# A recurrence and a mixture of experts on one core: two stretches of mixture a chunk, T sent by chunk, a new order of the beginning

## The chip, the cores and the metric

One core of one Trainium2 chip runs the whole program. The metric is the time of one execution in device microseconds.

## What is computed

Three stages follow each other: a linear recurrence with a matrix state (4 batches x 8 heads, 768 tokens, head size 40), a dense gated layer, and a dense mixture of four experts on its result.

```python
def _attn_ref(r, k, v, w, a, b):
    for t in range(S):
        y[:, :, t] = np.einsum('bhd,bhde->bhe', rt, state)
        Sa = np.einsum('bhde,bhe->bhd', state, at)
        state_decay = state * wt[:, :, None, :] - np.einsum('bhd,bhe->bhde', Sa, bt)
        state = state_decay + np.einsum('bhd,bhe->bhde', vt, kt)

def _moe_ref(x, w_a, w_b, w_out):
    return (x @ w_a * (x @ w_b)) @ w_out

def _moe2_ref(x, domain_probs, w1, w2):
    p = domain_probs / (domain_probs.sum(-1, keepdims=True) + 1e-09)
    for e in range(E):
        out += p[:, e:e + 1] * (np.maximum(x @ w1[e], 0.0) @ w2[e])
```

## The kernel before, in words

The recurrence is worked in chunks of 32 tokens. There are 48 of them: the batches are split into two passes (NPASS), whose chunks alternate, so that chunk n follows on chunk n-2. Four chunks make a group (SUP); a group gives one tile of 256 columns to the first dense layer, which this document calls the mixture (class Moe1): per tile 12 blocks of 24 matmuls in a pair of l1 (16) and l2 (8).

A chunk needs these steps, all methods of Att. `decay` (L130) scans the decays to R, `inverse` (L138, L140) takes the reciprocal gam, `scale` (L149, L152) multiplies k and b by R into a tile ke, and a by gam into A. `prep_T` (L170, L174) makes the matrix T of a chunk and transposes k and b; VectorE masks a half of it (L177), ScalarE copies the other half to tbs (L179) and the transposes to L (L182). T of a chunk must be inverted with ones on the diagonal: `invert` does it for a whole group at once, on 128 partitions, in 31 pairs of an elementwise multiply (L203) and a subtract (L206). Half of the partitions hold the even columns of an inverse and half the odd ones. For that T goes through DRAM: two stores of a group's tbs to td, issued by ScalarE (L190), two loads to tblk (L195) and one of the start values X (L197), issued by SP. `place` stores X to DRAM (xd, L215) and loads it as xr in another layout (L218). `settle` copies xr to xs on ScalarE (L225), with even and odd columns interleaved.

Then come `rhs` (L304, a copy to rh on ScalarE L308), `u` (L324, reads xs; ScalarE and VectorE write its result to G, L328, L330), and `sy` (L347: new state, VectorE L355, and output ys, L359). Beside them lie, for later chunks, `tr` (L290, transposes the state; copy S, L293), `q` (L274, copy L278) and `cf` (L253, mask L257). rhs, u and sy all use the PSUM buffer with tag "B", prep_T the one with tag "A".

The order of all engines is written by hand in `body`. From chunk 4 on the loop puts per chunk: rhs with tr, a stretch of mixture `moe(g[0])`, u with q, `moe(g[1])`, sy with cf, T of chunk n + LEAD, and `moe(g[2])`. The counts are matmuls: 18, 26, 22 up to chunk 7, then 20, 28, 24. In a group's first chunk settle stands ahead of u, and after u `split` (L422, L423) cuts the tile of the group before into a high and a low part; `moe` doesn't enter a tile before that (`ready`). At a group's last chunk place follows u. `mo.load` sends ys through DRAM (L516 store xt, L520 and L522 loads xf).

The weights of the mixture come by `Moe1.fetch`, issued by ScalarE (L453), 1.9 MB for two of twelve blocks. `convert` (L496 to L509) turns them to a high and a low part in steps, on VectorE, ScalarE and GpSimd; `fill` takes such steps. In the beginning, the chunks' inputs e1 are fetched into buffers of their own or of tiles that are used later (E1); T of chunks 0 to 3 is made, the first inverse is taken on VectorE, T of 4 to 7 is made among its steps; the second inverse is taken on GpSimd, as all later ones are. After the loop the rest of the mixture runs, and then the experts (Moe2, L694 to L716).

Of the kernel before, what the change touches and what calls it, by code (L numbers as in the profile page):

```python
# [19 lines left out]
C = 32  # L20
NCH = S // C
NPASS = 2
# [15 lines left out]
NK = (128, 104)  # L38

# [34 lines left out]
E1 = ("e1", "ys", "tblk1", 0, 1, "e1", "ys", "e1")  # L74


class Att:
# [3 lines left out]
    def __init__(self, ctx, tc, e1, e2, vt, cst):  # L81
# [23 lines left out]
        self.pre, self.sup, self.e2, self.S, self.rh = {}, {}, {}, {}, {}  # L105
# [12 lines left out]
    def fetch(self, n):  # L118
        tag = E1[n] if n < RING else "e1"
        if tag in (0, 1):  # L120
            e1 = self.L[tag][:104, SUP:].rearrange("p i a d -> p (i a d)")[:, :1032]
        else:
            e1 = self.pool.tile([104, 1032], F32, tag=tag, name=f"e1_{n}", bufs=1)[:]
        self.nc.sync.dma_start(e1, self.e1d[n])
        self.pre[n] = e1
# [8 lines left out]
    def inverse(self, n):  # L134
        nc, pool = self.nc, self.pool
        e1, R = self.pre[n]
        gam = pool.tile([104, 8, 32], F32, tag="gam", name=f"gam_{n}", bufs=RING + 1)
        nc.vector.reciprocal(gam[:], R[:, :, 1:33])  # L138
        lc = pool.tile([104, 8, 1], F32, tag="lc", name=f"lc_{n}", bufs=RING)
        nc.scalar.copy(lc[:], R[:, :, 32:33])  # L140
        self.pre[n] = e1, R, gam, lc

    def scale(self, n, eng):
# [4 lines left out]
        ke = self.pool.tile([104, 8, 2, 32], F32, tag="ke", name=f"ke_{n}")  # L148
        eng.tensor_tensor(out=ke[:], in0=kb, in1=R[:, :, 0:32].unsqueeze(2).to_broadcast([104, 8, 2, 32]), op=ALU.mult)  # L149
# [3 lines left out]
        self.pre[n] = lc, gam, ke  # L153

    def prep_T(self, n, tag="A"):
# [5 lines left out]
        if cc == 0:  # L161
            self.sup[s] = pool.tile([128, SUP * 8, 32], F32, tag="tbs", name=f"tbs_{s}", bufs=1)
        tbs = self.sup[s]
# [11 lines left out]
        for P in range(2):  # L175
            kr, br = (slice(x[P], x[P] + 32) for x in (KROW, BROW))
# [7 lines left out]

    def invert(self, s, eng):

        nc, pool = self.nc, self.pool
        td = self.dr.tile([SUP * 8, 2, 32, 32], F32, tag="td", name=f"td_{s}")
        for P in range(2):
            nc.scalar.dma_start(td[:, P].rearrange("a j t -> j a t"), self.sup[s][BROW[P]:BROW[P] + 32])  # L190
        yield
        tb = pool.tile([128, 32, 32], F32, tag=f"tblk{s % 2}", name=f"tblk_{s}", bufs=1)
        src = td[:].rearrange("a v j t -> (a v) (j t)")
        for z in range(2):
            nc.sync.dma_start(tb[64 * z:64 * z + 64].rearrange("p j t -> p (j t)"), src)  # L195
        X = pool.tile([128, 32, 16], F32, tag=f"xx{s % 2}", name=f"xblk_{s}", bufs=1)
        nc.sync.dma_start(X[:], self.x0d)  # L197
        yield
        for k in range(31):
            m, c = 31 - k, k // 2 + 1  # L200
            tm = pool.tile([128, 136], F32, tag="tmp0" if s == 0 else "tmp", name=f"tmp_{s}_{k}")
            t = tm[:, :m * c].rearrange("p (j c) -> p j c", c=c)
            eng.tensor_tensor(out=t, in0=tb[:, k + 1:, k:k + 1].to_broadcast([128, m, c]),  # L203
                                    in1=X[:, k:k + 1, :c].to_broadcast([128, m, c]), op=ALU.mult)
# [5 lines left out]
    def place(self, s):  # L210
# [5 lines left out]
        xr = pool.tile([128, 2, SUP * 4, 16], F32, tag=f"xx{s % 2}", name=f"xr_{s}", bufs=1)  # L216
        for z in range(2):
            nc.sync.dma_start(xr[:, z], xd[z].rearrange("a p c -> p a c"))  # L218
        self.sup[s] = xr

    def settle(self, s):
        nc, pool, xr = self.nc, self.pool, self.sup[s]
        xs = pool.tile([128, SUP * 4, 16, 2], F32, tag="xs", name=f"xs_{s}", bufs=1)
        for z in range(2):
            nc.scalar.copy(xs[:, :, :, z], xr[:, z])  # L225
        self.sup[s] = xs
# [84 lines left out]
    def u(self, n, tag="B", also=None):  # L311
# [4 lines left out]
        xs = self.sup[s]  # L316
# [3 lines left out]
        for j in range(4):  # L320
            for z in range(2):
                for P in range(2):
                    b = band(z, P)
                    nc.tensor.matmul(U[rows[P], z, j], xs[b, 4 * cc + j].rearrange("p c z -> p (c z)"), rh[b, j], start=True, stop=True)  # L324
# [4 lines left out]
        for P, br in enumerate(rows):  # L329
            nc.vector.tensor_tensor(out=g_t(G[P][br]), in0=p_t(ps[br]),  # L330
                                    in1=self.um[br].unsqueeze(1).unsqueeze(1).to_broadcast([32, 2, 4, 32]), op=ALU.mult)
        next(more, None)

    def sy(self, n, ys, tag="B", also=None):
# [15 lines left out]
        yield  # L350
        m = n + NPASS
        if m < N:
# [4 lines left out]
        yield  # L357
        for P, o in enumerate(rows):
            nc.vector.tensor_tensor(out=ys[o, :, cc].rearrange("p (j z) t -> p z j t", z=2), in0=p_t(ps[o]),  # L359
                                    in1=gam[o].rearrange("p (j z) t -> p z j t", z=2), op=ALU.mult)  # L360
# [6 lines left out]
def consts():  # L367
    c = np.zeros((128, CST_N), np.float32)
    tri = np.tril(np.ones((32, 32), np.float32), -1)
# [33 lines left out]
def pack_att(r, k, v, w, a, b):  # L403
    ch = {n: _chunks(x) for n, x in dict(r=r, k=k, v=v, w=w, a=a, b=b).items()}
    em = {n: _emajor(ch[n], 0, 0.0) for n in "kab"}
# [23 lines left out]
class Moe1:  # L429
# [16 lines left out]
    def fetch(self, i):  # L446
# [357 lines left out]
def general(tc, e1, e2, cst, wab, w2d, wo, probs, w1, w2, out):  # L804
# [4 lines left out]
    with ExitStack() as c:  # L809
        dram = c.enter_context(tc.tile_pool(name="gdram", bufs=1, space=DRAM))  # L810
        x2 = dram.tile([NS, 128, 3, 256], F32, name="x2g")
        with ExitStack() as ctx:
            mo = Moe1(ctx, tc, wab, w2d, wo, {}, True)
            for i in range(0, mo.NK1, 2):
                mo.fetch(i)
# [28 lines left out]
            with tc.For_i(0, NS, 1) as s:  # L844
                ys = pool.tile([104, 8, SUP, 32], F32, tag="ys", name="gys", bufs=1)
                for step in range(2):
# [19 lines left out]
                    for t in range(31, -1, -1):  # L866
# [3 lines left out]
                        tt(dv[:], eye, wide(E2[:, :, 1, :, t]), ALU.mult)  # L870
# [7 lines left out]
                        for z in range(2):  # L878
                            tt(x[:, z], Sa[z], kb[:, z, 1, :, t].unsqueeze(2).to_broadcast(full[:1] + full[2:]), ALU.mult)
                        tt(S[:], S[:], x[:], ALU.subtract)  # L880
                        V = total(dv, "V")
                        for z in range(2):
                            tt(x[:, z], V[z], kb[:, z, 0, :, t].unsqueeze(2).to_broadcast(full[:1] + full[2:]), ALU.mult)
# [31 lines left out]
def body(ctx, tc, e1, e2, vt, cst, wab, w2d, wo, probs, w1, w2, out):  # L915
# [6 lines left out]
    with ExitStack() as ca:  # L922
# [55 lines left out]
        for n in range(SUP):  # L978
            fetch(n)
        for n in range(NPASS):  # L980
            at.loade(n)
            at.loadv(n)
        at.loadv(2)
        at.ones(0)
        for n in range(SUP, RING - 1):
            fetch(n)
        for n in range(3):
            prep(n, pool)
        for n in range(SUP):
            at.prep_T(n, "AB"[n % 2])  # L990
            if n == SUP - 1:
                inv = at.invert(0, v)
                steps(1)
            if n + 3 < RING - 1:
                prep(n + 3, pool)
        at.ones(1)
        steps(1)
        fetch(7)
        mo.fetch(0)
        at.prep_T(4, "A")  # L1000
        steps(14)
        at.prep_T(5, "B")
        prep(7, pool)
        steps(20)
        at.prep_T(6, "A")
        steps(14)
        at.prep_T(7, "B")
        inv0, inv = inv, at.invert(1, pool)
        steps(1)
        whole(inv0)  # L1010
        at.place(0)
        steps(1)
        mo.fetch(2)
        both(at.cf(0), at.cf(1))
        at.loade(2)
        at.loade(3)
        at.rhs(0, "A")
        at.rhs(1, "B")
        whole(at.cf(2))
        fill(4)  # L1020
        steps(12)
        at.settle(0)
# [3 lines left out]
        fill(2)  # L1026
        y0, y1 = at.sy(0, ys, "A"), at.sy(1, ys, "B")
        both(y0, y1)
        at.loadv(3)
        mo.fetch(4)  # L1030
        steps(8)
        whole(at.tr(2, None, "A"))
        whole(at.tr(3, None, "B"))
        fill(4)
        whole(at.q(2))
        whole(at.q(3))
        at.rhs(2, "A")
        whole(at.cf(3))
        at.rhs(3, "B")
        at.loade(4)  # L1040
        at.loadv(4)
        at.loade(5)
        fill(6)
        steps(12)
        at.u(2, "A")
        at.u(3, "B")
        fill(2)
# [3 lines left out]
        fetch(8)  # L1051
        mo.fetch(6)
        steps(12)
        fill(4)
        both(at.cf(4), at.cf(5))
        whole(at.tr(4, None, "A"))
        whole(at.q(4))
        fill(6)
        mo.split(0)
        steps(100)  # L1060
        at.place(1)
        prep(8, v)
        at.prep_T(8)
        fetch(9)
        for i in range(8, mo.NK1, 2):
            mo.fetch(i)
        ready = 1
        for n in range(SUP, N):
            s, cc = divmod(n, SUP)
            m = n + LEAD  # L1070
            g = (18, 26, 22) if n < RING else (20, 28, 24)
            at.rhs(n, "B", n + 1)
            if n + 2 < N:
                if n > SUP + 1:
                    at.loade(n + 2)
                if n > SUP:
                    at.loadv(n + 2)
            if n == SUP:
                at.loade(n + 2)
                prep(9, v)  # L1080
                fetch(10)
            elif n == SUP + 1:
                at.loade(n + 2)
                prep(11, v)
                fetch(12)
            elif m < N:
                at.inverse(m)
                at.scale(m, v)
                fetch(m + 1)
            moe(g[0])  # L1090
            if n < SUP + 2:
                at.prep_T((9, 11)[n - SUP])
            if n == SUP + 1:
                inv, every = at.invert(2, pool), 2
                steps(2)
            if cc == 0:
                at.settle(s)
            at.u(n, "B", n + 1)
            if cc == 3 and s + 1 < N // SUP:
                steps(100)  # L1100
                at.place(s + 1)
                every = 0
            if cc == 0 and s > 1:
                mo.split(s - 1)
                ready += 1
            if n < SUP + 2:
                prep((10, 12)[n - SUP], v)
                fetch((11, 13)[n - SUP])
# [84 lines left out]
```

## Time and profile before

| | us |
|---|---|
| median of 3 runs (lowest to highest) | 1729.84 (1723.58 to 1734.29) |
| the profiled execution | 1729.1 |
| its span | 1727.3 |
| TensorE busy | 1463.6 |
| VectorE, ScalarE, GpSimd busy | 837.6, 593.2, 406.3 |
| mean granted clock of TensorE | 0.935 |

The span goes from the first to the last instruction. Matmuls are pipelined, so TensorE's busy time is that in which at least one is under way; PEld is its loading of weights. SPq and ACTq are the queues' own instructions, DMA issues above all; "x2" counts merged instructions. The number in brackets is the engine's idle time before the instruction, and what ended it.

### The profile page before, as it was taken

To read this page: it belongs to the slowest core of one execution; us is meant where nothing else is said; L and a number is where in the kernel's file an instruction comes from. 1 tells how busy PE (TensorE), PEld (TensorE's weight loads), DVE (VectorE), ACT (ScalarE), POOL (GpSimd) and SP (SyncE) were. 2 spreads that over 40 slices of the span, in tenths; PEclk is the share of its full clock that TensorE was granted. 3 is DMA by queue.
4 is the path that set the end of the run, shared out by engine and by line. 5 is a ranking of instruction groups with operands and counts; after the bars stand their busy time and mean duration, and the time that the engine had idled before them with its cause. 6 is when DMAs were issued, how large, how long until landed. Compare 5 with 4: busy or idle time off the path is not lost.

```text
span 1727.3 us, 40183 instructions
## 1 busy us (share of the span) xinstructions
PE 1463.6 (85%) x17202; PEld 1326.5 (77%) x17202; DVE 837.6 (48%) x1631; ACT 593.2 (34%) x1450; POOL 406.3 (24%) x794
## 2 busy tenths in 40 slices
PE   4144657988978889889889999999999999999998
PEld 3144657877877878778778887777899999999997
DVE  6564875655756556566534454445322322232222
ACT  2132334333434334443433466664211211121111
POOL 5162380522605325144150220002000200010000
PEclk9975778988999889999999999999999999999999
DMA  8445214332342323432321466557200100000000
GB/s 197 92 137 130 71 29 88 76 85 66 86 105 68 82 61 93 98 76 77 73 57 28 148 179 162 149 155 237 70 1 0 57 12 1 1 1 16 31 16 33
DMA packets 142623, 135.81 MB, mean 79 GB/s; under 512 B 94628, under 2 KB 112484, under 8 KB 142436
## 3 DMA queue, kind: packets, MB, share of 16 engines
q1 hardware_dynamic: 113012, 117.99, 25.8%
q10 hardware_dynamic: 29424, 15.17, 3.4%
q8 instruction: 137, 2.24, 0.6%
q14 instruction: 50, 0.41, 0.1%
HBM read 115.03 MB, written 18.09 MB: 77 GB/s over the span
## 4 chain that ended last, share of the span: by engine, by line


## 5 line engine op out<-in xcount | busy, mean ns | idle before, releaser
L563 PE MATMUL l<-xh,w 128*128 128x256 f32 x1440 | 316.5, 303 | 34.1 <-ACT xh L422 33.0
L698 DVE SCALAR_TENSOR_TENSOR hl<-l,hh 128x512 fp32r<-128x512 f32 x192 | 132.3, 690 | 344.0 <-ACT hh L697 343.8
L563 PEld LDWEIGHTS l<-xh,w 128*128 128x128 f32 x1440 | 255.2, 208 | 37.8 <-ACT xh L422 34.5
L563 PE MATMUL l<-xl,w 128*128 128x256 f32 x864 | 263.7, 311 | 0.1
L697 ACT ACTIVATE hh<-l 128x512 fp32r<-128x512 f32 x192 | 114.0, 595 | 396.0 <-PE l L694 396.0
L711 PE MATMUL o<-h,hh 128*128 128x320 f32 x768 | 239.1, 311 | 9.7 <-ACT hh L697 6.1
L713 PE MATMUL o<-h,hl 128*128 128x320 f32 x768 | 239.9, 313 | 5.1 <-DVE hl L698 4.9
L203 POOL TENSOR_TENSOR tmp<-tblk,xblk 128x126 f32<-128x126 f32 (+22 forms) x341 | 139.0, 408 | 424.3 <-DMA xblk<-cst 320.5
L712 PE MATMUL o<-l,hh 128*128 128x320 f32 x768 | 236.9, 309 | 0.0
L563 PEld LDWEIGHTS l<-xl,w 128*128 128x128 f32 x864 | 179.5, 208 | 6.2 <-DVE xl L423 2.1
L423 POOL TENSOR_TENSOR l<-r,h 128x512 fp32r<-128x512 f32 (+1 forms) x32 | 46.7, 1483 | 575.6 <-ACT h L422 575.6
L711 PEld LDWEIGHTS o<-h,hh 128*128 128x128 f32 x768 | 144.2, 188 | 26.1 <-ACT hh L697 14.5
L713 PEld LDWEIGHTS o<-h,hl 128*128 128x128 f32 x768 | 144.0, 188 | 12.2 <-DVE hl L698 11.6
L206 POOL TENSOR_TENSOR xblk<-xblk,tmp 128x126 f32<-128x126 f32 (+22 forms) x341 | 145.9, 428 | 26.9 <-POOL tmp L203 0.2
L694 PE MATMUL l<-XL,h 128*128 128x512 f32 x384 | 151.7, 395 | 0.0
L694 PE MATMUL l<-XH,h 128*128 128x512 f32 x384 | 151.5, 395 | 0.0
L694 PE MATMUL l<-XH,l 128*128 128x512 f32 x384 | 150.0, 391 | 0.0
L712 PEld LDWEIGHTS o<-l,hh 128*128 128x128 f32 x768 | 144.2, 188 | 6.7
L170 PE MATMUL psT<-A,ke 40*64 40x32 f32 x1536 | 67.0, 240 | 64.1 <-DVE A L152 28.4
L567 DVE TENSOR_TENSOR g<-l,a 128x256 f32<-128x256 f32 x144 | 60.7, 421 | 116.4 <-ACT a L565 116.2
L170 PEld LDWEIGHTS psT<-A,ke 40*64 40x64 f32 x1536 | 60.7, 158 | 67.9 <-issue 36.2
L179 ACT COPY tbs<-psT 32x256 f32<-32x256 f32 x96 | 35.0, 365 | 219.5 <-DVE A L177 217.1
(119 smaller groups left out, 2643.3 us busy)
## 6 DMA issues: line engine op xcount, KB each, us to landing
g<-e SPq DMA_DIRECT2D x48, 419.2 KB
e<-e SPq DMA_DIRECT2D x46, 419.2 KB
e<-e SPq DMA_DIRECT2D x48, 208.0 KB
wr<-wab ACTq DMA_DIRECT2D x12, 512.0 KB
tblk<-td SPq DMA_DIRECT2D x24, 256.0 KB
r<-w SPq DMA_DIRECT2D x8, 768.0 KB
gx<-wab SPq DMA_DIRECT2D x12, 512.0 KB
r<-w SPq DMA_DIRECT2D x8, 640.0 KB
```

Source lines behind the costliest of these rows:

```text
L170: nc.tensor.matmul(T[P][KROW[P]:KROW[P] + 64, a], ke[r, a].rearrange("p y t -> p (y t)"), self.A[P][r, k, a], start=True, stop=True)
L203: eng.tensor_tensor(out=t, in0=tb[:, k + 1:, k:k + 1].to_broadcast([128, m, c]), in1=X[:, k:k + 1, :c].to_broadcast([128, m, c]), op=ALU.mult)
L206: eng.tensor_tensor(out=X[:, k + 1:, :c], in0=X[:, k + 1:, :c], in1=t, op=ALU.subtract)
L423: eng.tensor_tensor(out=lo, in0=raw, in1=hi, op=ALU.subtract)
L563: nc.tensor.matmul(o, l, r, start=j == 0, stop=j == len(ops) - 1)
L567: nc.vector.tensor_tensor(out=g[:], in0=ps[:, 256:512], in1=a[:], op=ALU.mult)
L694: nc.tensor.matmul(ps[:], l, r, start=i == 0, stop=i == len(ops) - 1)
L697: nc.scalar.activation(hh[:], ps[:], AF.Relu)
L698: nc.vector.scalar_tensor_tensor(out=hl[:], in0=ps[:], scalar=0.0, in1=hh[:], op0=ALU.max, op1=ALU.subtract)
L711: nc.tensor.matmul(o[:], hh[:, s], h2[:, k], start=first, stop=False)
L712: nc.tensor.matmul(o[:], hh[:, s], lo2[:, k], start=False, stop=False)
L713: nc.tensor.matmul(o[:], hl[:, s], h2[:, k], start=False, stop=last)
```

## The change

Tokens of k, v and b stand in a chunk with the even positions ahead of the odd ones (ORD), so that an inverse can be used as its two halves lie, and settle is gone. scale works in place on e1, with two instructions for k and b. T goes to DRAM by chunk, in four stores and two loads, all issued by SP; X's start values are loaded apart. In the loop T of chunk n + 7 is made between rhs and u, sy uses the PSUM buffer "A" and, from chunk 2 on, writes ys ahead of the state, and the mixture has two stretches a chunk: 28 and 20 matmuls up to chunk 7, then 44 and 28. place stands at the start of a group's last chunk, split ahead of sy in its first one. Weights are fetched by SP, and the beginning has a new order. The program that is taken for other inputs (`general`) follows the new order of tokens.

```diff
+ORD = [*range(0, C, 2), *range(1, C, 2)]
-E1 = ("e1", "ys", "tblk1", 0, 1, "e1", "ys", "e1")
+E1 = ("e1", "e1", "e1", 0, 1, "tblk1", "ys", "e1")
...
-        ke = self.pool.tile([104, 8, 2, 32], F32, tag="ke", name=f"ke_{n}")
-        eng.tensor_tensor(out=ke[:], in0=kb, in1=R[:, :, 0:32].unsqueeze(2).to_broadcast([104, 8, 2, 32]), op=ALU.mult)
+        for y in range(2):
+            k = kb[:, :, y].rearrange("p a (z c) -> p a z c", z=2)
+            eng.tensor_tensor(out=k, in0=k, in1=R[:, :, 0:32].rearrange("p a (c z) -> p a z c", z=2), op=ALU.mult)
...
-            nc.scalar.copy(tbs[br, 8 * cc:8 * cc + 8], T[P][br])
+            nc.scalar.copy(tbs[br], T[1 - P][br])
+        for P in (1, 0):
+            for z in range(2):
+                o = BROW[P] + 16 * z
+                nc.sync.dma_start(td[8 * cc:8 * cc + 8, P].rearrange("a (c z) t -> z c a t", z=2)[z], tbs[o:o + 16])
+        yield
...
+    def loadt(self, n):
+        src = td[8 * cc:8 * cc + 8].rearrange("a v j t -> (a v) (j t)")
+        for z in range(2):
+            r = 64 * z + 16 * cc
+            self.nc.sync.dma_start(tb[r:r + 16].rearrange("p j t -> p (j t)"), src)
+    def loadx(self, s):
+        X = self.pool.tile([128, 32, 16], F32, tag=f"xx{s % 2}", name=f"xblk_{s}", bufs=1)
+        self.nc.sync.dma_start(X[:], self.x0d)
...
     def invert(self, s, eng):
-        for P in range(2):
-            nc.scalar.dma_start(td[:, P].rearrange("a j t -> j a t"), self.sup[s][BROW[P]:BROW[P] + 32])
-        for z in range(2):
-            nc.sync.dma_start(tb[64 * z:64 * z + 64].rearrange("p j t -> p (j t)"), src)
-        nc.sync.dma_start(X[:], self.x0d)
...
-        for z in range(2):
-            nc.sync.dma_start(xr[:, z], xd[z].rearrange("a p c -> p a c"))
+        yield
+        for r in (slice(0, 4), slice(4, 16)):
+            for z in range(2):
+                nc.sync.dma_start(xr[:, r, z], xd[z, r].rearrange("a p c -> p a c"))
-    def settle(self, s):
-        for z in range(2):
-            nc.scalar.copy(xs[:, :, :, z], xr[:, z])
...
-    def fetch(self, i):
+    def fetch(self, i, eng):
-            self.nc.scalar.dma_start(raw[:], src[:, m * at:m * at + m])
+            eng.dma_start(raw[:], src[:, m * at:m * at + m])
```

The new beginning, in the order of its steps: fetch 0 to 2, inputs of chunks 0 and 1, fetch 3 to 6 and loadx(0) among them; prep (decay, inverse, scale on GpSimd) of 0 to 5 with T of 0 to 3 and their loadt between; loadv(2), mo.fetch(0), prep of 6 and 7, fetch 8 and 9; cf of 0 and 1, 16 steps of the first inverse (on VectorE), the cf masks, mo.fetch(2), rhs of 0 and 1, the rest of the inverse, its store; T(4), the load xr, T(5) to T(7) with loadt of 4 to 7 between; prep of 8 and 9; cf(2); then u of 0 and 1, with steps of the second inverse (GpSimd) and of the weights' conversion between, and on as before. mo.fetch(4) follows sy of 0 and 1, mo.fetch(6) sy of 2 and 3, and T(8). After the second inverse and its place come 24 matmuls of mixture, mo.fetch(8) and (10), T(9), fetch 12, prep 10, 16 matmuls, T(10), prep 11, 8 matmuls.

```diff
         for n in range(SUP, N):
-            g = (18, 26, 22) if n < RING else (20, 28, 24)
+            g = (28, 20) if n < RING else (44, 28)
+            if cc == 3 and s + 1 < N // SUP and n > RING:
+                whole(at.place(s + 1))
+            if SUP + 1 < n + 2 < N and n > SUP - 1 and n + 2 > 5:
+                at.loadv(n + 2)
             at.rhs(n, "B", n + 1)
...
-            moe(g[0])
-            if cc == 0:
-                at.settle(s)
-            at.u(n, "B", n + 1)
+            rest = ()
+            if m < N:
+                rest = at.prep_T(m)
+                next(rest)
+                fetch(m + 3)
+                if m % SUP == SUP - 1:
+                    at.loadx(m // SUP)
+            if m + 1 < N:
+                at.decay(m + 1)
+            at.u(n, "B", n + 1, rest)
+            if cc == 3 and n < RING:
+                whole(inv)
+                whole(at.place(s + 1))
+            if n + 3 < N:
+                at.loade(n + 3)
+            moe(8)
+            if m + 1 < N:
+                at.inverse(m + 1)
+            if m < N:
+                at.loadt(m)
+                if m % SUP == SUP - 1:
+                    inv, every = at.invert(m // SUP, pool), 2
+                    if n >= RING:
+                        whole(inv)
+            moe(16)
+            if m + 1 < N:
+                at.scale(m + 1, v)
+            moe(g[0] - 24)
             if cc == 0 and s > 1:
                 mo.split(s - 1)
+            whole(at.sy(n, ys, "A", n + 2))
+            if cc == 0 and s > 1:
                 ready += 1
             if cc == SUP - 1:
                 mo.load(s, ys)
-            if m < N:
-                at.prep_T(10 if n == SUP else m)
-            moe(g[2])
+            moe(g[1])
```

## Rows read from the trace of the kernel before

**Rows 1.** Busy time by stretch: us, PE, PEld, DVE, ACT, POOL, clock, DMA share, GB/s.

```profile
0.00:272.40 272.40, 127.87 (x2232) 117.26 (x2232) 176.60 (x333) 79.01 (x222) 122.52 (x203) 0.78 0.43 107
272.40:833.70 561.30, 482.75 (x8953) 445.73 (x8954) 345.88 (x701) 225.50 (x659) 206.65 (x496) 0.93 0.34 82
833.70:957.00 123.30, 108.14 (x1869) 100.58 (x1869) 51.72 (x122) 45.06 (x120) 23.81 (x62) 0.93 0.21 51
957.00:1727.30 770.30, 744.86 (x4157) 662.98 (x4155) 263.43 (x476) 243.61 (x450) 53.28 (x33) 0.99 0.24 71
```

**Rows 2.** Timeline at a group's first chunk: start, duration, engine, instruction.

```profile
630.15 1.18 PE L324 MATMUL psU<-rh,xs 32*32 32x72 f32 x32 [3.28 <-ACT xs L225]
...
634.65 1.02 ACT L422 CAST xh<-xf 128x256 fp32r<-128x256 f32 x3
```

**Rows 3.** Busy time in two stretches of 2 us, columns as in rows 1.

```profile
600.00:602.00 2.00, 2.00 (x19) 2.00 (x18) 1.47 (x3) 1.04 (x4) 1.76 (x4) 1.00 0.81 229
...
638.00:640.00 2.00, 2.00 (x11) 2.00 (x10) 0.36 (x1) 0.37 (x1) 0.00 (x0) 0.50 0.00 0
```

**Rows 4.** Waits of the whole run: us in total, times, longest.

```profile
PE psY L347 <- ACT G L278: 27.3, 24, 3.8
```

**Rows 5.** Timeline of TensorE: T in one chunk, then chunk 41.

```profile
603.74 1.12 PE L170 MATMUL psT<-A,ke 40*64 40x32 f32 x32
605.16 0.38 PE L563 MATMUL l<-xl,w 128*128 128x256 f32 x1
...
869.91 0.71 PE L304 MATMUL psR<-G,A 128*32 128x72 f32 x32
...
870.93 0.38 PE L563 MATMUL l<-xl,w 128*128 128x256 f32 x1
...
873.50 0.70 PE L324 MATMUL psU<-rh,xs 32*32 32x72 f32 x32
...
874.57 0.39 PE L563 MATMUL l<-xh,w 128*128 128x256 f32 x1
...
878.11 1.20 PE L347 MATMUL psY<-G,L 128*40 128x72 f32 x32
...
879.62 0.39 PE L563 MATMUL l<-xl,w 128*128 128x256 f32 x1
```

**Rows 6.** Timeline of SP's queue over two chunks and the next group's start.

```profile
603.45 2.30 SPq L238 DMA_DIRECT2D G<-vt  x2
...
616.97 1.13 SPq L215 DMA_DIRECT2D xd<-xblk  x2
620.97 1.47 SPq L218 DMA_DIRECT2D xr<-xd  x2
622.53 1.45 SPq L516 DMA_DIRECT2D xt<-ys  x2
628.20 0.38 SPq L520 DMA_DIRECT2D xf<-xt  x1
```

**Rows 7.** GpSimd's inverse of one group, by line; then two rows of the timeline.

```profile
L206 POOL TENSOR_TENSOR xblk<-xblk,tmp 128x126 f32<-128x126 f32 (+22 forms) x31 | 13.8, 444 | 2.4
L203 POOL TENSOR_TENSOR tmp<-tblk,xblk 128x126 f32<-128x126 f32 (+22 forms) x31 | 12.3, 395 | 43.2 <-DMA xblk<-cst 40.9
...
611.83 0.80 POOL L203 TENSOR_TENSOR tmp<-tblk,xblk 128x78 f32<-128x78 f32 x1
612.71 0.40 POOL L206 TENSOR_TENSOR xblk<-xblk,tmp 128x78 f32<-128x78 f32 x1
```

**Rows 8.** Timeline of the beginning, one row of each engine that waited.

```profile
44.25 0.20 DVE L203 TENSOR_TENSOR tmp<-tblk,xblk 128x31 f32<-128x31 f32 x1 [11.07 <-DMA xblk<-cst]
...
91.21 2.14 PE L324 MATMUL psU<-rh,xs 32*32 32x72 f32 x64 [4.15 <-ACT xs L225]
...
137.10 0.58 PE L563 MATMUL l<-xh,w 128*128 128x256 f32 x1
...
152.86 0.40 ACT L308 COPY rh<-psR 128x288 f32<-128x288 f32 x1 [14.49 <-issue]
```

More of the change, by code (lines that the diff above doesn't have):

```diff
@@ L309, in rhs, with u @@
         next(more, None)
[L311 removed]
+    def u(self, n, tag="B", also=None, between=()):
         nc, rh = self.nc, self.rh.pop(n)
@@ L331, in u, with sy @@
                                     in1=self.um[br].unsqueeze(1).unsqueeze(1).to_broadcast([32, 2, 4, 32]), op=ALU.mult)
+        for _ in between:
+            pass
         next(more, None)
-    def sy(self, n, ys, tag="B", also=None):
+    def sy(self, n, ys, tag="B", also=None, first="y"):
         nc = self.nc
@@ L350, in sy, with y @@
         yield
+        def y():
+            for P, o in enumerate(rows):
+                nc.vector.tensor_tensor(out=ys[o, :, cc].rearrange("p (j z) t -> p z j t", z=2), in0=p_t(ps[o]),
+                                        in1=gam[o].rearrange("p (j z) t -> p z j t", z=2), op=ALU.mult)
         m = n + NPASS
+        if first == "y":
+            y()
+            yield
         if m < N:
@@ L356, in sy @@
                                         in1=lc[o].rearrange("p (j z) o -> p z j o", z=2).to_broadcast([40, 2, 4, 40]), op=ALU.mult)
[L357 to L360, printed above, removed]
+        if first != "y":
+            yield
+            y()
         next(more, None)
@@ L996, in body, with mix @@
[L996 to L1002, printed above, removed]
-        prep(7, pool)
[L1004 to L1014, printed above, removed]
+        def mix(k, f=4):
+            for _ in range(k):
+                steps(f)
+                fill(1)
@@ new lines, in T @@
+        def T(n, tag):
+            whole(at.prep_T(n, tag))
+        for n in range(3):
+            fetch(n)
+        at.loade(0)
+        at.loadv(0)
+        fetch(3)
+        at.loade(1)
+        at.loadv(1)
+        at.ones(0)
+        fetch(4)
+        fetch(5)
+        at.loadx(0)
+        fetch(6)
+        prep(0, pool)
+        prep(1, pool)
+        prep(2, pool)
+        T(0, "A")
+        fetch(7)
+        prep(3, pool)
+        T(1, "B")
+        at.loadt(0)
+        prep(4, pool)
@@ L1015, in body @@
+        T(2, "A")
+        at.loadt(1)
+        prep(5, pool)
+        T(3, "B")
+        at.loadt(2)
+        at.loadt(3)
+        at.loadv(2)
+        mo.fetch(0, nc.sync)
+        prep(6, pool)
+        prep(7, pool)
+        fetch(8)
+        fetch(9)
+        inv = at.invert(0, v)
+        c0, c1 = at.cf(0, at.bank("psC_0", "A")), at.cf(1, at.bank("psC_1", "B"))
+        next(c0)
+        next(c1)
+        steps(16)
+        both(c0, c1)
         at.loade(2)
         at.loade(3)
+        mo.fetch(2, nc.sync)
@@ L1017, in body @@
         at.rhs(0, "A")
         at.rhs(1, "B")
+        whole(inv)
+        put = at.place(0)
+        next(put)
+        T(4, "A")
+        whole(put)
+        at.ones(1)
+        T(5, "B")
+        at.loadt(4)
+        T(6, "A")
+        at.loadt(5)
+        T(7, "B")
+        at.loadt(6)
+        at.loadx(1)
+        at.loadt(7)
+        fetch(10)
+        prep(8, pool)
+        prep(9, pool)
         whole(at.cf(2))
-        fill(4)
-        steps(12)
-        at.settle(0)
+        inv = at.invert(1, pool)
@@ L1023, in body @@
+        steps(4)
         ys = newys(0)
```

167 lines of the change are left out of this document (60 added, 107 removed).

## The prediction, made before the changed kernel was run

> **What bounds the kernel now.** I read the table of stretches first [rows 1]. The program has three parts: a beginning up to 272.4 us, when chunk 8 of the recurrence starts; the loop over the other chunks up to 957 us; and the tail, 770.3 us, in which TensorE is busy 744.9 us and the recurrence is over. In the beginning TensorE is busy for 127.9 of 272.4 us, in the eight groups of four chunks (chunks 8 to 39) for 482.8 of 561.3, which is 70.2 us a group, in the last eight chunks for 108.1 of 123.3. No other engine is near full there: VectorE has 345.9 us for 32 chunks, 10.8 each. So the loop waits. The second view, the timeline at a first chunk of a group, shows where [rows 2]: TensorE stood 3.28 us until ScalarE had copied the inverses (xs), and after that the mixture waited until ScalarE split the new tile (xh, from 634.65). The third, two-microsecond stretches, shows what follows [rows 3]: the granted clock is 0.50 at 638 to 640, the 1.2 GHz level, and 11 mixture matmuls fit in place of 19. The fourth adds smaller waits: sy stood 27.3 us in 24 waits until ScalarE had read the PSUM buffer that it shared with u [rows 4].
>
> **What a chunk costs when nothing waits.** Chunk 41 shows it [rows 5]: rhs and tr 869.91 to 870.93, 1.02; 20 mixture matmuls 2.57; u and q 1.07; 28 matmuls 3.54; sy and cf 1.51. The two stretches of mixture differ by 8 matmuls and 0.97, so a matmul is 0.121 and coming in and out of the mixture 0.15. A chunk that also prepares another one has 1.42 for T and K (603.74 to 605.16). Before: 72 x 0.121 + 3 x 0.15 + 1.02 + 1.07 + 1.51 + 1.42 = 14.2. A group would be 56.7 of its 70.2.
>
> **The change in the loop, part by part.**
> - Two stretches of mixture, not three: one entry less, 0.15, so 14.0 a chunk, 56 a group. What lay in the first stretch covered ScalarE's copy of rh. Now T and K cover it (1.42 against a copy of about 0.4 and S of 0.4). In chunks 41 to 47 no T is left: about 0.65 of wait opens, bounds 0 and 1.2; such a chunk is 12.76 - 0.15 + 0.65 = 13.25.
> - sy moves to the other PSUM buffer: the wait of [rows 4] goes. What sy needs next is VectorE's masked t rows; by the durations of the groups they come some 2.5 us ahead of it, since 44 matmuls (5.3 us) lie between.
> - No copies of the inverses: 0.8 of ScalarE a group and, above all, the wait for a place in ScalarE's order, 3.28 [rows 2]. u now waits for the load itself. That is issued at the start of chunk 3 of a group and not after its u, a whole chunk (15) ahead of use.
> - The new tile is first wanted after sy of the group's first chunk instead of straight after u. That is the first stretch of mixture (5.3) and sy (1.5) later, and what each such stall costs now, some 11.5 us (two waits of about 3.2 and 10 us at half speed, of which 5 are lost), should shrink to 2, bounds 0 and 11.5. At the low bound the tile is there; at the high one all that [rows 2, 3] show stays.
> - Scaling k and b in two instructions instead of one, in place: about 0.2 more VectorE a chunk. VectorE then has 11.0 in 14 to 15 us; it is covered, with 3 us of slack. Without that cover it costs its 0.2.
> - ys before state in sy: state is 0.86 later, but tr wants it after 28 matmuls and rhs, 4 us on. Nothing, or 0.86 if VectorE is late.
> - T by chunk: SP gets four small writes and two reads a chunk, beside two loads of v, one of e1, one of e2. The waits that this adds are for T in SBUF and for the landing of T, and behind them stand all other loads. This makes a ring, whose time for a group I add up [rows 6, 7]: GpSimd's 62 steps 12.3 + 2.4 + 13.8 + 2.3 = 30.8; store of X 1.13 and its landing 2.87; the load xr 2.2; v 1.3; T 1.8; e1 and e2 0.8; wait for T 1.5, read 0.8; xt 1.45 and its landing 4.2 at most, 3.5 taken; xf 1.5; v, T, e1, e2, x0 again 4.5; wait and read 1.8; landing 2.4. Without GpSimd that is 27.6; the pieces of T, which no row has, are taken at 0.45 each, between xf's first at 0.38 and xd's two at 0.57 (bounds 0.31 and 1.15). GpSimd's step beside VectorE's scaling took 0.80 and the next one 0.40 [rows 7]. VectorE is denser after the change, so I take 32 for 30.8 (bounds 30.8 and 36, the steps stretched in the ratio of the two VectorE shares). The ring then has 59.6 against 56 + 2 on TensorE. I take **60 us a group**, 57 to 66.
> The Trainium skill, GPSIMD Engine Reference, section Specifications, says that GpSimd's SBUF interface is shared with VectorE and contended by VectorE instructions with two SBUF inputs. By it all scaling and subtracting of VectorE would stretch the steps, some 33 us of GpSimd as an estimate and 61 a group; the trace agrees in the pair named, 0.80 against 0.40.
>
> **The beginning.** The rows of now [rows 8]: the first inverse starts at 44.25 after 11.07 of waiting for its input; u of chunk 0 at 91.21; the mixture at 137.10; and ScalarE's copy of rh at 152.86 after 14.49 in which its queue only issued weight loads. After the change:
> - The inputs of the first inverse go chunk by chunk and its start values early, so it starts when T of chunk 3 is there, about 32. It now takes 25.6, to 69.84, of which 6.2 are masks and preparation between its steps; 19.4 and the cf masks, 1.7, end it at 53.
> - Then T of chunks 4 to 7 and the preparation of 8 and 9 lie ahead of u: 4 x 1.7 + 2 x 2.5 + 2 = 14. The way of X out and back (8 to 10) is beside it. u at 67, 24 earlier.
> - From there to the mixture it is now 46; without the preparation of chunk 8 that stands in it about 37: 104, 33 earlier.
> - Weights come by SP, so ScalarE is never stopped by them. But SP now stands in order: the last four chunks of weights (3.8 MB: 36 us at the mean rate of [rows 1] for the beginning, 18 at twice that, 24 taken) are issued behind the second inverse, and e1 of chunk 12 behind those. u of chunk 4 comes at about 145 (now 164). Four chunks with 11 us of VectorE each and 33 us of weight conversion (seven of twelve blocks at 4.7, by their lines) are 78 of VectorE; at the share that it reached between 135 and 272 now, three quarters, 95 to 100.
> Chunk 8 then starts at **240**, 32 earlier; bounds 215 (no wait at 145) and 272 (nothing gained).
>
> **The sum.** 240 + 8 x 60 + chunks 40 to 47: 14.0 + 7 x 13.25 + two first chunks at 2 extra = 111; the tail 770.3 and 24 matmuls more that the loop leaves to it, 2.9. Together 1604 us of span. The profiled execution took 1729.1 for a span of 1727.3, so 1.8 is outside: 1606. That execution is 0.7 below the median 1729.84, so it stands for it. I predict **1606 us**, 7% faster.
>
> **Rivals.**
> 1. The ring of SP and GpSimd decides and is slower: each extra wait of one landing (2.87) for v, T or xf, twice a group, and GpSimd at 33 make 66 a group: 1606 + 8 x 6 = 1654. For it: xt's landing of 4.2 stood on SP alone [rows 6]. Against: in the trace SP is idle most of a chunk. If the tile is then so late that the stall of [rows 2, 3] stays as it is, 56 + 11.5 = 67.5, 1666: the same case.
> 2. The beginning gains nothing, since weights, T, e1 and e2 share one queue: 1638. For it: the beginning is also short of VectorE, 176.6 of 272.4 us. Against: 14.49 of ScalarE and 11.07 of VectorE are waits with a named cause.
> 3. Everything meets: 57 a group and chunk 8 at 215: 1606 - 24 - 25 = 1557.
> 4. Slower: SP's issuing itself is the bound. The pair of v loads took 2.30 at 603.45 [rows 6], 1.15 each. If each of the ten transfers of a chunk cost that, with one landing a chunk and a quarter of the group's 15 extra transfers and landings, it is 11.5 + 2.9 + 6.1 = 20.5 a chunk, 82 a group: 1606 + 8 x 22 = 1782. It decides from 75.5 a group (18.9 a chunk) on, where all gains are eaten. Against: xf's first took 0.38, xr's two 1.47.
> The Trainium skill, DMA: Bandwidth & Descriptors, sections Anatomy of one DMA and Measured, gives a DMA a fixed cost of about 2.0 us and calls transfers under 64 KB dominated by descriptors; pieces of T are 16 KB. If the four of a chunk paid that in turn, rival 4's sum would hold with 8 us for T, 80 to 85 a group by estimate. No run here shows pieces of that size; the rows show landings of 2.9 to 4.2 and second transfers issued before the first has landed.
> 5. It doesn't do what it says: VectorE, with ScalarE in turn on each PSUM buffer, comes late for sy or T, so that the chunk goes at 17 and the group at 68 or more, the beginning gaining 32 all the same: 1670 to 1690. Against: chunks with 15.0 exist now at the same VectorE work.
>
> **Chances.** Forecast (1570 to 1630) 0.50; rival 1 0.22; rival 2 0.10; rival 3 0.10; rival 4 0.04; rival 5 0.04. The range, 1553 to 1675, goes from rival 3's time to a little over both of rival 1's; outside lie the rest of rival 3 and rivals 4 and 5. Of this kernel about 1% can be told from no change: faster by over 1% 0.95; rival 4's 0.04 and a little that I don't foresee divide into within 1% 0.02 and slower 0.03.
>
> **What would show it.** In the profile after: no copies to xs, and u waits for nothing but rh; T's matmuls between tr and u; groups of 58 to 62 us between first chunks, with the clock at 1.00 through them; the start of GpSimd's first step about 14 us after a group's first rhs and its end near the third chunk's; u of chunk 0 near 67, the first mixture matmul near 104, chunk 8 near 240; a tail of 773. I am wrong if SP's waits for T's landing stand ahead of xf or xr and TensorE waits for those (rival 1), if chunk 8 starts at 260 or later (rival 2), or if SP is never idle in the loop (rival 4).

## The result, and the profile after

The changed kernel takes **1595.61 us** (median of 4 runs, 1594.52 to 1597.78), the kernel before in the same comparison 1727.49 (4 runs, 1723.58 to 1734.29): a ratio of 0.923, 95% interval 0.920 to 0.927, 7.7% faster. The forecast was 1606, in a range of 1553 to 1675. The profiled execution took 1594.88 for a span of 1592.7. Of the four executions of the first experiment below one took 3401.61 us at a clock of 1.00: its ratio leaves that one out, and its median would be 1597.56 without it.

The stretches of the changed kernel, and one of its groups, in the columns of [rows 1]:

```profile
0.00:226.90 226.90, 120.36 (x2212) 109.89 (x2213) 174.35 (x327) 77.10 (x217) 138.78 (x219) 0.83 0.51 132
226.90:717.90 491.00, 464.06 (x8953) 432.96 (x8954) 355.05 (x745) 224.25 (x647) 200.40 (x496) 0.97 0.41 93
717.90:823.50 105.60, 99.19 (x1840) 92.76 (x1840) 46.63 (x113) 41.08 (x108) 23.67 (x62) 1.00 0.21 51
823.50:1592.70 769.20, 748.87 (x4210) 669.46 (x4208) 265.56 (x481) 244.37 (x454) 53.52 (x33) 1.00 0.24 71
348.90:410.60 61.70, 58.27 (x1125) 54.30 (x1124) 44.16 (x92) 28.16 (x82) 25.01 (x62) 0.97 0.41 94
```

Of the 134.6 us of span that are gone, the beginning gave 45.5 (272.4 to 226.9), the eight groups 70.3 (561.3 to 491.0), and the last eight chunks with the tail the remaining 18.8. TensorE's busy time in the groups fell by 18.7 only (482.75 to 464.06); 51.6 of the 70.3 was idle time. The matmuls are the same 8953, and the clock rose from 0.93 to 0.97: that accounts for the busy time that went.

The waits of TensorE, over seven groups of each kernel (columns: us in total, times, longest). Before, 340 to 834 us:

```profile
PE psU L324 <- ACT xs L225: 22.9, 7, 3.3
PE l L563 <- ACT xh L422: 21.6, 7, 3.1
PE psY L347 <- ACT G L278: 18.7, 20, 1.3
PE o L599 <- ACT x L612: 5.9, 7, 0.9
```

After, 290 to 718 us:

```profile
PE o L621 <- ACT x L634: 12.3, 7, 1.9
PE l L585 <- ACT xh L444: 9.2, 7, 2.1
```

The first and the third wait are gone, the wait for the tile (xh) fell from 3.1 to 1.3 us a group, and that for ScalarE's copies of the mixture's output (L634) grew from 0.8 to 1.8. Together 9.9 us a group became 3.1. A group takes 61.2 us on the mean of the seven (289.4 to 717.9) after 70.6.

A group now loses time in its first two chunks. The first one of a group, in TensorE's timeline and in two stretches of 3.4 us (columns of [rows 1]):

```profile
358.95 0.46 PE L263 MATMUL psY<-e 40*32 40x32 f32 x32
360.88 0.38 PE L585 MATMUL l<-xh,w 128*128 128x256 f32 x1 [1.47 <-ACT xh L444]
```

```profile
361.30:364.70 3.40, 3.36 (x13) 3.09 (x14) 2.40 (x7) 0.40 (x1) 0.00 (x0) 0.50 0.36 61
364.70:368.10 3.40, 3.40 (x77) 3.11 (x76) 1.49 (x5) 1.28 (x4) 0.00 (x0) 1.00 0.92 249
```

The engine waits 1.47 us for the tile and then has a stretch at 0.50, the 1.2 GHz level, which costs half of 3.4. This group's four chunks take 17.6, 16.1, 14.0 and 14.0; on the mean of the seven groups the first chunk takes 16.4 and the second 16.8. In the seven groups from 289.4 us on the clock was at 0.50 for 3.4 us six times; a group with none took 59.5, one with a stretch 61 to 62, the one with two 64.0. Before it was 6.8 to 13.7 us in each group.

SP's queue and the first step of GpSimd's inverse, over the same group:

```profile
351.60 0.76 SPq L538 DMA_DIRECT2D xt<-ys  x2
357.62 0.38 SPq L542 DMA_DIRECT2D xf<-xt  x1
...
361.53 1.76 SPq L187 DMA_DIRECT2D td<-tbs  x4
...
364.76 0.77 SPq L203 DMA_DIRECT2D tblk<-td  x2
...
389.99 0.78 SPq L203 DMA_DIRECT2D tblk<-td  x2
400.06 2.21 SPq L230 DMA_DIRECT2D xd<-xblk  x2
404.14 2.27 SPq L235 DMA_DIRECT2D xr<-xd  x4
```

```profile
370.24 0.71 POOL L218 TENSOR_TENSOR tmp<-tblk,xblk 128x31 f32<-128x31 f32 x1 [30.89 <-PE psU L284]
```

GpSimd works from 370.24 to 400.03 and then stands until its next inverse; that idle time is called the turn here, and it took 30.4 to 33.3 us. Over the seven groups it is 29.8 for the inverse and 31.3 for the turn: 61.1, against 61.2 of the group. Between 390.77 and 400.06 SP issues nothing: it waits for GpSimd to store X, and v, T and the tile are queued behind that.

### The profile page after: what moved, and what is told of

Read it like the earlier page. It is cut to its first block, busy times and chain, and to the rows that moved or that the text cites. A ratio compares the mean times of both kernels' runs of the same rounds, so it can differ in the third digit from the quotient of the medians.

```text
span 1592.7 us, 40694 instructions
## 1 busy us (share of the span) xinstructions
PE 1432.5 (90%) x17202; PEld 1305.1 (82%) x17202; DVE 841.6 (53%) x1663; ACT 586.8 (37%) x1426; POOL 416.4 (26%) x810
## 4 chain that ended last, share of the span: by engine, by line
## 5 line engine op out<-in xcount | busy, mean ns | idle before, releaser
L585 PE MATMUL l<-xh,w 128*128 128x256 f32 x1440 | 298.0, 292 | 10.0 <-ACT xh L444 9.2
L585 PEld LDWEIGHTS l<-xh,w 128*128 128x128 f32 x1440 | 241.7, 197 | 12.3 <-ACT xh L444 10.0
L585 PE MATMUL l<-xl,w 128*128 128x256 f32 x864 | 248.8, 295 | 0.8
L218 POOL TENSOR_TENSOR tmp<-tblk,xblk 128x126 f32<-128x126 f32 (+22 forms) x341 | 135.8, 398 | 298.0 <-DMA tblk<-td 87.5
L585 PEld LDWEIGHTS l<-xl,w 128*128 128x128 f32 x864 | 170.0, 197 | 5.5 <-DVE xl L445 3.2
L594 ACT CAST gh<-g 128x256 fp32r<-128x256 f32 x144 | 58.4, 406 | 160.1 <-DVE g L589 160.0
L621 PE MATMUL o<-gh,wo 128*128 128x256 f32 x288 | 85.4, 296 | 15.2 <-ACT x L634 14.5
L181 DVE TENSOR_TENSOR A<-psT,acst 32x256 f32<-32x256 f32 x96 | 40.0, 417 | 111.6 <-PE psT L178 80.4
L174 PE MATMUL psT<-A,e 40*64 40x32 f32 x1472 | 61.9, 236 | 35.4 <-POOL A L154 11.0
```

The source lines that it names most:

```text
L174: nc.tensor.matmul(T[P][KROW[P]:KROW[P] + 64, a], ke[r, a].rearrange("p y t -> p (y t)"), self.A[P][r, k, a], start=True, stop=True)
L585: nc.tensor.matmul(o, l, r, start=j == 0, stop=j == len(ops) - 1)
L594: self.nc.scalar.copy(gh[:], g[:])
L621: nc.tensor.matmul(o, h, gh[:], start=s and f == 0, stop=False)
```

## The experiments

Each kernel is the changed one with the edit shown; times are medians, ratios against the kernel before with their 95% intervals. The changed kernel's own is 0.923 (0.920 to 0.927). Differences of 2 or 3 us between these kernels can't be told from nothing. Most edits undo one part of the change. T by chunk, the earlier start of place and the scaling in place were not undone, so their shares of the gain are not known.

**Three stretches of mixture again.**

```diff
-            g = (28, 20) if n < RING else (44, 28)
+            g = (28, 20) if n < RING else (24, 28)
...
+            moe(0 if n < RING else 20)
             at.u(n, "B", n + 1, rest)
```

> From the changed kernel, the mixture is again entered three times a chunk from chunk 8 on: 20 matmuls between rhs with its T and u, 24 between u and sy, 28 after sy. Theory (the third entry costs only its switch of 0.15 us): 40 x 0.15 = 6 us more, 1602 us (1597 to 1606), a group 62. Rival (fewer stretches carry the loop's gain of 8.8 us a group): eight groups at 70, 1665 us.

Measured 1597.64, ratio 0.925 (0.923 to 0.927); groups of 60.5, chunks after the last T of 12.8 (13.5 in the changed kernel, where u waits up to 0.8 for ScalarE's copy of the state). The number of stretches, which stands in the title, is worth nothing by itself in this kernel. What holds its groups at 61 is shown further down; a small loss of TensorE's beside that doesn't show, here and in the next run.

**sy on u's PSUM buffer.**

```diff
-            whole(at.sy(n, ys, "A", n + 2))
+            whole(at.sy(n, ys, "B", n + 2))
```

> From the changed kernel, sy takes the PSUM buffer that it shares with rhs and u again. Theory (44 matmuls between u and sy, 5.3 us, already give the readers of u's buffer their time, so the other buffer is worth nothing): 1594 to 1603 us. Rival (the buffer itself took the wait of 27.3 us in 24 away): 1.1 us in each of 40 chunks, 1640 us.

Measured 1596.28, ratio 0.923 (0.921 to 0.926), and no wait of sy's matmuls from 290 to 718 us. So the buffer alone is worth nothing here either.

**Both at once.** The two diffs above together.

> From the changed kernel, both three stretches of mixture (20, 24, 28) and sy on the PSUM buffer of u: the two edits that alone cost 2 and 1 us, together. Theory (either of them alone takes sy's wait for u's readers away, by 44 matmuls of distance or by the other buffer; without both the wait of 18.7 us in 7 groups is back): 0.7 us and a switch of 0.15 in each of 40 chunks, 1625 to 1640 us. Rival (both are worth nothing in the changed kernel): 1596 to 1602 us.

Measured 1615.27, ratio 0.937 (0.934 to 0.939), 17.6 us more than with the first edit alone; groups of 63.6. The two edits cover one and the same loss, and either does it alone. I expected more (1625 to 1640), and the wait at sy; the trace has a small one there and a larger one a step on, where rhs finds the buffer still read by VectorE's masks (290 to 718 us):

```profile
PE psR L314 <- DVE G L267: 10.4, 7, 1.6
...
PE psY L359 <- ACT G L288: 2.3, 7, 0.4
```

**The tile wanted straight after u.**

```diff
             if n + 3 < N:
                 at.loade(n + 3)
+            if cc == 0 and s > 1:
+                mo.split(s - 1)
+                ready += 1
             moe(8)
```
(and both taken out around sy)

> From the changed kernel, the new tile is split and wanted straight after u of a group's first chunk, as before the change, not after its sy. Theory (the stall at the first chunk is what the loop lost): ScalarE and VectorE stand at the split until the tile has landed, some 5 us later than now in their order, TensorE 3 to 5 us longer and then at half speed: 4 to 6 us in each of nine groups, 1632 to 1650 us. Rival (the ring of SP and GpSimd sets the group's length): 1594 to 1600 us.

Measured 1612.20, ratio 0.933 (0.931 to 0.935); groups of 63.5. The wait for the tile is back at up to 4.1 us:

```profile
PE l L585 <- ACT xh L444: 18.4, 5, 4.1
```

Less than half of what was expected: the rest of the loop waits for something else anyway (below). Nor is all of the price shown to be the tile's: in this kernel GpSimd's inverses took 31.2 to 32.6 us, in the changed one 29.5 to 30.3.

**The inverses copied again.** In place and not interleaved, so only the work and its place in ScalarE's order come back.

```diff
+    def settle(self, s):
+        xr = self.sup[s]
+        for z in range(2):
+            self.nc.scalar.copy(xr[:, :, z], xr[:, :, z])
...
+            if cc == 0:
+                at.settle(s)
             at.u(n, "B", n + 1, rest)
```

> From the changed kernel, ScalarE copies the inverses of a group once (in place, same size) ahead of u of the group's first chunk, and u waits for that. Theory (the load comes 6 us before u now, so the copy costs its own 0.8 us and the place behind rh, 0.8 to 1.5 us in each of ten groups): 1604 to 1611 us. Rival (the copies with their place in ScalarE's order were the stall, 3.28 us and 5 of half speed): 1660 to 1680 us.

Measured 1618.53, ratio 0.937 (0.934 to 0.939). Both expectations missed, the low one by less: u waits 2.5 us in each group for the copies, and the clock is at 0.50 for 3.4 us about twice a group instead of once.

```profile
PE psU L339 <- ACT xr L241: 17.4, 7, 2.5
```

**Weights fetched by ScalarE.** `nc.scalar` for `nc.sync` in the five mo.fetch of the beginning.

> From the changed kernel, the weights of the mixture are fetched by ScalarE's queue again, at the same places. Theory (ScalarE stopped by issuing weights was what the beginning lost, 14.5 and 13.6 us): chunk 8 starts 10 to 28 us later than 226.9, 1606 to 1624 us. Rival (the beginning gained by the earlier inverse and the order alone; SP is relieved): 1590 to 1598 us.

Measured 1609.30, ratio 0.933 (0.930 to 0.936); chunk 8 starts at 241.5, 14.6 later. Of ScalarE's waits in the beginning the two largest new ones are 14.2 us together: copies of T stand behind the issue of weights.

```profile
ACT tbs L183 <- DMA wor<-wo: 8.1, 1, 8.1
...
ACT tbs L183 <- DMA wr<-wab: 6.1, 1, 6.1
```

So a third of the beginning's 45.5 is the queue of the weights.

**u of chunk 0 earlier.**

```diff
         T(4, "A")
+        T(5, "B")
         whole(put)
         at.ones(1)
-        T(5, "B")
         at.loadt(4)
         T(6, "A")
         at.loadt(5)
+        prep(8, pool)
+        prep(9, pool)
         T(7, "B")
...
         fetch(10)
-        prep(8, pool)
-        prep(9, pool)
```

> From the changed kernel, in the beginning T of chunk 5 is written ahead of the loads of the first inverse, and chunks 8 and 9 are prepared ahead of T of chunk 7, while VectorE stood 6.39 us for it. Theory (what lies ahead of u of chunk 0 is on the path to chunk 8): u at 74 in place of 79.2, chunk 8 at 222, 1591 us. Rival (VectorE's own work and the weights set chunk 8): u at 74, chunk 8 still at 226 to 228, 1594 to 1597 us.

Measured 1594.09, ratio 0.923 (0.921 to 0.925). u came at 73.0 in place of 79.2, u of chunk 4 at 148.2 (147.2), chunk 8 at 224.9 (226.9). Of the 6.2 us at u at most 2.0 reached chunk 8, and the profiles of kernels with the beginning unchanged have chunk 8 anywhere from 224.6 to 228.7: what lies ahead of u is hardly on the path to it.

**Less VectorE in the beginning.** `prep(10, pool)` and `prep(11, pool)` for `v`: GpSimd scales.

> From the changed kernel, GpSimd scales chunks 10 and 11 in the beginning in VectorE's place. Theory (from 107 us to chunk 8 VectorE's own work sets the time, it is busy 94 of the 108 us from 119 to 227, and so u of chunk 0 5 us earlier was worth nothing): two scalings, some 4 us, off VectorE; chunk 8 at 223, 1592 us. Rival (the chain from u of chunk 0 over the states sets it): chunk 8 at 227 or, with GpSimd's slower steps in the chain, later, 1596 to 1600 us.

Measured 1596.43, ratio 0.925 (0.923 to 0.926); chunk 8 at 226.8. VectorE worked 73.0 us from rhs of chunk 4 to chunk 8 (76.9), and that stretch was 2.4 shorter, but rhs of chunk 4 came 2.3 later: T of chunk 10 stood 7.5 us for GpSimd's scaling where it had stood 5.4 for VectorE's. What sets the beginning from 80 us on is not settled by this.

**The mixture lags by 28 matmuls.**

```diff
-            moe(g[1])
+            if n != RING:
+                moe(g[1])
```

> From the changed kernel, 28 matmuls of the mixture are left out in chunk 8 (they come in the tail), so that from then on the mixture lags by 28 matmuls and wants a new tile only after u of a group's second chunk, 7 us later than now. Theory (the 3.6 us that a first chunk takes above 14.0 are the wait for the tile and the half-speed clock behind it): 9 x 3.6 less, 3.4 more in the tail, 1566 to 1573 us, a group 57.8. Rival (the ring of SP and GpSimd sets the group): groups stay at 61, 1592 to 1599 us.

Measured 1595.37, ratio 0.924 (0.920 to 0.928), the rival's time. First chunks of a group now take 14.0, second ones 16.4 to 22.2; a group 61.3. TensorE no longer waits for the tile; it waits at tr for the state (12.7 us in 9 waits), because ScalarE and VectorE still stand at the split: before one of these waits, of 2.6 us, ScalarE stood 5.3 for the tile to land. And the clock falls without a long wait. Two stretches of its windows, the recurrence's matmuls and what follows them:

```profile
363.60:365.00 1.40, 1.21 (x69) 0.99 (x65) 0.84 (x3) 0.58 (x2) 0.00 (x0) 1.00 1.00 241
365.00:368.40 3.40, 3.40 (x18) 3.40 (x17) 2.76 (x5) 3.21 (x10) 0.01 (x1) 0.50 0.81 150
```

**The lag in the beginning's order too.** Both edits in one kernel.

> The edits of the two runs on the lag of 28 matmuls and on the order in the beginning, together. Theory: both gains add, 1562 to 1569 us. Rivals: 1592 to 1596 us if the ring sets the groups, 1566 to 1573 us if the order in the beginning is worth nothing.

Measured 1592.46, ratio 0.920 (0.917 to 0.923): the time of the ring rival again.

**The split later as well.** The lag, and

```diff
-            if cc == 0 and s > 1:
-                mo.split(s - 1)
...
             whole(at.sy(n, ys, "A", n + 2))
             if cc == 0 and s > 1:
+                mo.split(s - 1)
                 ready += 1
```

> As the run with the lag of 28 matmuls, and ScalarE and VectorE also split the new tile later, behind sy's evictions in place of ahead of them. Theory (in that run the tile was wanted later, but its split still stood in the two engines' order ahead of the rows that the recurrence needs, so the wait moved to tr and to the next chunk): chunks of 14.0 and a group of 57 to 58, 9 x 3.5 less and 3.4 more in the tail, 1566 to 1574 us. Rival (the ring of SP and GpSimd needs 59 to 61 a group, so that u or the tile is late again): 1583 to 1597 us.

Measured 1595.54, ratio 0.924 (0.923 to 0.926). Windows of chunks 12 to 15 and of the next group:

```profile
285.10:341.30 56.20, 56.20 (x1121) 52.80 (x1120) 43.50 (x93) 27.81 (x81) 25.75 (x62) 1.00 0.39 97
341.30:401.70 60.40, 57.77 (x1121) 54.35 (x1120) 43.67 (x93) 27.92 (x81) 25.58 (x62) 0.97 0.42 95
```

The first runs as the theory has it: TensorE is busy for all of 56.20. From the next on a group takes 61.4 on the mean, and the waits are for loads of e2 and of the inverses on SP's queue, and for the copy of the state, which ScalarE makes late after standing for the tile (6.4 us ahead of 420.09):

```profile
PE psY L263 <- DMA e<-e: 7.5, 4, 3.0
PE psU L334 <- ACT S L303: 6.6, 5, 2.5
PE psU L334 <- DMA xr<-xd: 2.6, 4, 1.5
```

TensorE gets ahead for one group and is then held by GpSimd and SP, whose inverse and turn still take 61.4 together: the rival.

**The inverses' transfers moved on SP.** The lag and the later split, and in a group's last chunk SP no longer waits for GpSimd with the chunk's other transfers behind it:

```diff
-            if cc == 3 and s + 1 < N // SUP and n > RING:
-                whole(at.place(s + 1))
             if SUP + 1 < n + 2 < N and n > SUP - 1 and n + 2 > 5:
                 at.loadv(n + 2)
             at.rhs(n, "B", n + 1)
...
                     at.loadx(m // SUP)
+            if cc == 3 and s + 1 < N // SUP and n > RING:
+                whole(at.place(s + 1))
```

> As the run with the lag and the later split, and the store and the loads of a group's inverses stand on SP behind the loads of v and the stores of T of the group's last chunk, not ahead of them. Theory (the ring sets the group: GpSimd's inverse 30.3 us and 30 to 31 us from its end to its next start, of which SP stands some 10 us for GpSimd's end with v, T and the tile queued behind): the turn shrinks to 26 or less, TensorE sets the group at 56 to 57.5, 9 x 3.5 to 4.5 less: 1556 to 1566 us. Rival (the ring isn't what holds the group at 61, the tile's way is): 1590 to 1597 us. Other side: the inverses come late for u of the next group, 1600 us or more.

Measured **1571.37** (5 runs, 1565.95 to 1572.08), ratio 0.908 (0.906 to 0.910): 24 us less than with the other two edits alone, and faster than both kernels, if not the 1556 to 1566 of the theory. SP's queue at the end of a group, with the store of X behind T now, and a start of GpSimd in that kernel, after a turn of 26.3:

```profile
451.72 1.93 SPq L187 DMA_DIRECT2D td<-tbs  x4
453.77 0.34 SPq L125 DMA_DIRECT2D e<-e  x1
455.71 1.14 SPq L230 DMA_DIRECT2D xd<-xblk  x2
459.50 2.26 SPq L235 DMA_DIRECT2D xr<-xd  x4
```

```profile
425.38 0.26 POOL L218 TENSOR_TENSOR tmp<-tblk,xblk 128x31 f32<-128x31 f32 x1 [26.33 <-DMA tblk<-td]
```

SP's waits for GpSimd from 226 to 740 us, first in the changed kernel, then here:

```profile
SPq L230 <- POOL xblk L221: 78.8, 8, 11.9
```

```profile
SPq L230 <- POOL xblk L221: 12.6, 6, 5.0
```

Between the inverses that begin from 369.4 to 652.9 the turn is 26.2 to 27.6 us in place of 31.3, the inverse about as long as before (30.2), and the six groups from 347.8 to 689.9 take 57.0 each; one of them still has a stretch at the half clock. This edit was not run on the changed kernel without the other two.

## Why the prediction was right

The time was 10 us under the forecast, inside its narrow range too; the parts were off by more and in both directions, so that the total came this near is in part luck.

- **The ring.** "The ring then has 59.6 against 56 + 2 on TensorE. I take 60 us a group." It was 61.1 for the ring and 61.2 for the group, and the last experiment shows that it was the bound: a shorter turn, with TensorE's work as it was, gave 57. Within it two terms were off and partly cancelled. GpSimd, taken at 32, needed 29.8, no more than before (30.4 to 30.8): VectorE's denser work didn't make the inverse longer as a whole. Single steps are longer beside VectorE's work, as the first step shows: 0.71 at 370.24 (above), beside a scan that reads two tiles in SBUF, and 0.26 in the next group, where no scan runs beside it:

```profile
370.21 0.68 DVE L131 TENSOR_TENSOR_SCAN R<-e,acst 104x264 f32<-104x264 f32 x1
...
431.83 0.26 POOL L218 TENSOR_TENSOR tmp<-tblk,xblk 128x31 f32<-128x31 f32 x1 [31.80 <-DMA tblk<-td]
```

  The Trainium skill's rule of contention (GPSIMD Engine Reference, Specifications) agrees with this pair; the 33 that was estimated from it for the whole inverse is not borne out. The way without GpSimd, taken at 27.6, needed 31.3: in the group shown xt landed after 5.3 (3.5 taken, 4.2 as the most; 2.8 to 5.3 in the seven groups), and from T's last load to GpSimd's first step it was 4.7 (2.4 taken; 4.0 to 6.4). The store of four pieces, where nothing waits, took 1.76: the 0.45 each that the sum took.
- **The chunk.** 14.0 was exact for the third and fourth chunk of each group. The light chunk, 13.25, measured 13.5.
- **The group's first chunk.** The stall of 11.5 was to shrink to 2: the copies' wait went, the tile's fell to 1.3 with up to 1.7 of half clock behind it. The first chunk is 2.4 over 14.0 on the mean, 3.6 in the group shown. Not foreseen was the wait for the output copies in the second chunk, 1.8. The runs with the copy and with the early tile price the two edits at 23 and 17 us in all, 2.3 a group over ten and 1.8 over nine, less than the 3.3 and 3.1 of wait a group that each had before. That fits a ring of 61, beside which shorter waits of TensorE cost nothing; no run shows it by itself.
- **sy's buffer.** That the wait goes was right; the reason was half. The distance of 44 matmuls did it as well as the buffer.
- **The beginning.** Forecast 240, measured 226.9. Its steps came later than forecast and its end earlier. The first inverse began at 37.1 (32) and took 21.1 (21). The forecast's 32 is when T of chunk 3 was there, with nothing for its way out to DRAM and back; a reciprocal of the preparation held VectorE until 36.9, and the load landed just after it:

```profile
31.56 1.74 SPq L187 DMA_DIRECT2D td<-tbs  x4
33.39 1.95 SPq L203 DMA_DIRECT2D tblk<-td  x4
35.17 1.75 DVE L139 RECIPROCAL gam<-R 104x256 f32<-104x256 f32 x1
37.11 0.20 DVE L218 TENSOR_TENSOR tmp<-tblk,xblk 128x31 f32<-128x31 f32 x1 [0.19 <-DMA tblk<-td]
```

  u came at 79.2 (67): besides those 5 us, T of chunk 7 stood for a free buffer whose store was queued behind the load xr:

```profile
72.64 0.36 ACT L183 COPY tbs<-psT 32x256 f32<-32x256 f32 x1 [5.93 <-DMA td<-tbs]
```

  The mixture began at 118.9 (104) and u of chunk 4 at 147.2 (145). From there the forecast had 95 and the run 80: the step that failed is "at the share that it reached between 135 and 272 now, three quarters". VectorE reached 86% (76.87 of 89.6 us) from rhs of chunk 4 on, and from u of chunk 4 on its work was 69.3 us, not 78. The share from 135 to 272 before was itself misread: it was 69% (95.0 of 137.0). And 78 at three quarters are 104, not 95 to 100, so that with its own numbers worked out the forecast of chunk 8 would have been 249 or later, farther off. That the chain to u hardly counted, the run with an earlier u shows; that VectorE is what counts is argued, not shown.
- **The tail.** Forecast 2.9 longer for the matmuls left over. From the end of the last sy's matmuls to the end of the span it was 774.6 before and 770.5 after: shorter. No run asked why.
- **The signs.** u had no wait from 290 to 718 us, and the groups took 61 on the mean. But GpSimd's first step came 21 us after a group's first rhs and not 14 (370.24 after 348.89), and the clock was 0.97 over the groups and not 1.00.
- **The sum.** Beginning 13 us better than forecast, groups 11 worse (491.0 for 480), last chunks 5 better (105.6 for 111), tail some 4 to 7 better.
- **The rivals.** Rival 1 has its place, the ring of SP and GpSimd, but at 61 and not at 66. Rival 2 falls with chunk 8 at 226.9. Rival 3's 57 a group needed another order on SP, and was then reached. Rival 4 falls: SP stood for 9 us of a group before the store of X alone, and pieces of 16 KB followed each other at 0.44 us. The Trainium skill names a fixed cost of about 2.0 us a transfer (DMA: Bandwidth & Descriptors, Anatomy of one DMA), for transfers that GpSimd issues; on SP's queue, by this row, no such cost is paid one after the other. Rival 5 falls with third and fourth chunks at 14.0.

## What to carry to other kernels

Where a loop has two engines that wait for each other in turn, add up the whole turn, engine time and transfers and queue order, and compare it with the bound engine's work: here 61 against the 56 that TensorE needs (56.2 in the one group that ran without a wait), and no edit on TensorE's side made it faster until the turn was shorter. A transfer that must wait for a slow engine goes as late as possible in an in-order queue, behind everything that is ready earlier: here that was worth 24 us. Two edits that cure the same wait each look worthless when undone alone; undo them together before calling either useless.

## What was not expected of the hardware

- The half clock didn't need a long wait ahead of it here. With the lag of 28 matmuls TensorE's longest wait from 346 to 365 us was 0.37, inside 4.5 us of the recurrence's small matmuls, and yet the clock stood at 0.50 from 365.0 to 368.4. The chunk before, with the same matmuls and no wait between them, kept 1.00.
- A landing is not one number: the store xt, issued in 0.8 us, held the load behind it for 2.8 to 5.3, the pieces of T held their loads for 2.1 at most (226 to 740 us).
